# A gated-recurrence block with an MLP on one core: f of the second pair issued from ScalarE's hardware queue, and a new order of the whole program

## The chip, the cores and the metric

The kernel runs on one core of one Trainium2 chip. The metric is the device time of one execution in microseconds; the median of three runs of the kernel before is 179.96 us (179.03 to 180.66).

## What is computed

Two parts follow one another. The first is a recurrence with a gate, for 4 sequences of 768 tokens and 8 heads of width 48; the second is an MLP on the 3072 rows of the result.

```python
f = 1.0 / (1.0 + np.exp(-f_logit))
for t in range(S):
    state = f[:, :, t, :, None] * state + np.einsum('bhd,bhe->bhde', k[:, :, t], v[:, :, t])
    y[:, :, t] = np.einsum('bhd,bhde->bhe', q[:, :, t], state)
...
h = x @ w_in                                  # 3072 x 384 by 384 x 2048
out = (h * (1.0 / (1.0 + np.exp(-h)))) @ w_out  # by 2048 x 384
```

All inputs and the output are float32 in HBM. The kernel computes in bf16 with float32 accumulation.

## The kernel before

The recurrence is done in chunks of 128 tokens. Inside a chunk it becomes masked products of q and k, scaled by running products of f, and between chunks a state of 48 x 48 per head is handed on. There are 24 chunks; the kernel takes them two at a time, as 12 **pairs** (0 to 11). Pairs 0 to 3 hold the first two chunks of one sequence ("T", tokens interleaved, two halves of 64), pairs 4 to 11 one chunk each of two sequences ("N").

Each pair goes through the same steps, and each step is one word in a long string, `PLAN`. A word such as `qg.1.0:G:3` is the step `qg` of pair 1, part 0, on engine G, into buffer 3 of its class. The order of the words is the order of the program: each engine executes its own words in that order, and semaphores do the rest. The letters are P for TensorE (PE), A for ScalarE (ACT), V for VectorE (DVE), G for GpSimd (POOL), and S for SyncE (SP), which only issues DMAs. The steps are:

- `f`, `k`, `q`, `v`: loads of one input for one pair, 384 KB each, line 236; all are issued by SP. f of pair 0 comes in two halves.
- `E`, `L` (ACT): exp and log of f (lines 242, 246, 249). `cs` (PE): running sums (lines 310 to 320). `ia`, `a`, `al` (ACT): exp of them (lines 322, 264, 324).
- `ki`, `qg` (DVE or POOL): k and q times those factors (line 327).
- `tq` (PE) and `qkc` (ACT or DVE): transpose through PE and copy out of PSUM (lines 334, 184/186), or in their place `qkD`: a DMA transpose on SP's queue (line 346).
- `sc` (PE): scores (355, 359). `at` (DVE): mask (363). `vb`: v to bf16 (184/186). `y`, `yi` (PE): the chunk's output (271, 376, 380). `d` (PE), `sd`, `su`: the state handed on (283, 397; 401 or a copy; 407 on POOL).
- `yc`: copy of y out of PSUM. Then `yT` (PE, 388) and `xc` (a copy) transpose it for the MLP, or in their place `yD`, a DMA transpose on SP's queue (392).
- `mi` (PE, 257): x times w_in, eight words for each pair, of six matmuls each; for pairs 0 and 1 each word is two half tiles `mi.P.j.0` and `mi.P.j.1` of 128 columns. `si` (ACT, 262): silu. `mo` (PE, 292): times w_out, four steps for each chunk, step n of which reads part n of w_out. `oc`: copy out. `so`: store, by SP or POOL (302, 304).
- `wi.n`, `wo.n` (214, 217): a quarter of w_in or w_out, issued by POOL with a conversion to bf16. `mi.P.j` reads quarter j/2 of w_in.
- `idle.512.9::7` (448): nine matmuls of 512 columns on zeros into PSUM bank 7, fillers on PE that compute nothing.

Eight PSUM banks and a few buffers of each class are all there is, so a word also waits for the last reader of the buffer that it names. The first four loads of the plan are issued ahead of the masks and constants. ACT has two table sets (exp/log and silu); where consecutive words of ACT need different sets, a table load of 1.28 us stands between (line 497).

The orders of the start that matter here, of the kernel before:

```
SP   f.0.1 f.0.0 f.1.0 k.0.0 q.0.0 q.1.0 k.1.0 v.0.0 f.2.0 v.1.0 k.2.0 q.2.0 v.2.0 f.3.0 f.4.0 k.3.0
POOL qg.1.0 wi.2 ki.1.0 wi.0 vb.0.0 su.0.0 wi.3 su.1.0 wi.1 wo.0 ki.2.0 su.1.1 wo.1 su.0.1 qg.2.1 qg.2.0 ki.2.1 wo.2 wo.3
ACT  E.0.1 L.0.1 E.0.0 L.0.0 E.1.0 ia.0.1 L.1.0 ia.0.0 a.0.1 al.0 a.0.0 ia.1.0 a.1.1 al.1 a.1.0 qkc.0.1 ia.1.1 vb.0.1 ...
PE   idle x10 cs.0 idle x9 cs.1 idle x1 tq.0 idle x4 sc.0 idle x3 tq.1.1 idle x2 tq.1.0 idle x2 d.0 sc.1.0 y.0 sc.1.1 d.1 cs.2 ... mi ...
```

Of the kernel before, what the change touches and what calls it, by code (L numbers as in the profile page):

```python
# [10 lines left out]
F32 = mybir.dt.float32  # L11
# [22 lines left out]

SLOTS = dict(f=4, k=6, q=6, v=6, e=2, lf=3, x=5, qk=5, vb=7, qkT=4, qkTT=2, atm=4, yb=3, xT=4, hT=4, sd=2, al=6, ob=6, pb=8, st0=1, st1=1, st2=1, st3=1)
# [3 lines left out]
f.0.1:S:0 f.0.0:S: f.1.0:S:1 k.0.0:S:0 q.0.0:S:0 E.0.1:A:0 L.0.1:A:0 E.0.0:A: L.0.0:A: q.1.0:S:1 idle.512.10::7 cs.0.1:P:0 cs.0.0:P:1 k.1.0:S:1  # L39
E.1.0:A:1 ia.0.1:A:0 L.1.0:A:1 v.0.0:S:0 ki.0.1:V:0 ia.0.0:A:1 idle.512.9::7 cs.1.0:P:2 a.0.1:A:2 ki.0.0:V:1 f.2.0:S:2 cs.1.1:P:3 al.0:A:0 a.0.0:A:3  # L40
qg.0.1:V: ia.1.0:A:4 qg.0.0:V: a.1.1:A:0 idle.512.1::7 tq.0.1:P:4 v.1.0:S:1 al.1:A:1 a.1.0:A:1 tq.0.0:P:5 qg.1.1:V:2 qkc.0.1:A:0 qg.1.0:G:3 qkc.0.0:V:
k.2.0:S:2 ia.1.1:A:2 wi.2:G: idle.512.4::2 sc.0.0:P:6,7 ki.1.1:V: sc.0.1:P:0,1 q.2.0:S:2 at.0.1.0:V:0 ki.1.0:G: idle.128.3::5 tq.1.1:P:2 vb.0.1:A:0
at.0.0.0:V:1 wi.0:G: at.0.1.1:V: v.2.0:S:2 idle.512.2::5 tq.1.0:P:4 qkc.1.1:V:1 vb.0.0:G:1 qkc.1.0:A: at.0.0.1:V: idle.512.2::6 d.0:P:5,3 E.2.0:A:0
vb.1.1:V:2 sc.1.0:P:0,6 vb.1.0:V:3 y.0:P:1,2 sd.0.0:A:0 at.1.0.0:V:2 L.2.0:A:2 sc.1.1:P:4,7 su.0.0:G:0 at.1.0.1:V: d.1:P:5,0 yc.0.0:A:0 at.1.1.0:V:3
# [4 lines left out]
si.0.5:A: mi.1.7.0:P:7 si.1.0:A:1 mi.0.7.0:P: qg.2.1:G:1 si.1.4:A: mi.0.6.1:P:3 mi.1.6.0:P:6 si.1.5:A: mi.1.6.1:P: si.0.0:A: qg.2.0:G: mi.1.7.1:P:
mi.0.6.0:P: mi.1.2.0:P:0 si.0.6:A: ki.2.1:G: mi.1.3.1:P:2 mi.0.3.1:P:4 si.1.1:A: f.4.0:S:0 mi.0.3.0:P: wo.2:G: mi.0.2.0:P:3 si.0.3:A: tq.2.0:P:5  # L50
si.1.7:A: wo.3:G: mi.1.2.1:P: mi.1.3.0:P: mi.0.2.1:P: tq.2.1:P:4 si.0.2:A: mo.1.1.0:P:7 qkc.2.1:V:0 si.1.6:A: mo.0.0.0:P:3 si.1.3:A: qkc.2.0:V:
si.0.7:A: mo.1.0.0:P:6 k.3.0:S:3 vb.2.0:V:4 si.1.2:A: sc.2.0:P:4,2 sc.2.1:P:5,1 at.2.0.0:V:1 mo.0.1.0:P:0 at.2.1.1:V:0 mo.1.0.1:P: at.2.0.1:V:
# [12 lines left out]
mi.3.4:P:6 qg.6.1:G:3 ia.5.1:A:4 yT.4.0:P:7 al.6.1:A:4 ia.5.0:A:2 d.4.1:P:1 mi.3.2:P:5 xc.4.0:V: E.7.0:A:1 sd.4.1:V:0 v.8.0:S:1 mi.4.0:P:3 ki.5.0:V:0
a.5.0:A:0 ki.6.1:V: mi.4.5:P:7 a.5.1:A:2 qg.5.0:G: ki.6.0:V: al.5.0:A:2 mi.3.0:P:1 mi.3.5:P:4 ki.5.1:G:2 si.3.0:A:3 mi.4.1:P:0 si.3.2:A: su.4.1:G:0
mi.4.6:P:1 si.3.5:A: mi.3.6:P:5 oc.2.0:V:5 qg.5.1:V: tq.5.0:P:4 si.3.6:A: mi.4.3:P:2 qkc.5.0:V:2 si.4.5:A:1 qkD.6.0:S:3 mi.3.1:P:5 si.4.0:A:
vb.6.0:V:2 vb.6.1:V:4 si.3.4:A: mi.4.4:P:7 vb.8.1:V:5 qkD.5.1:S:0 si.4.6:A: mi.4.2:P:4 si.4.1:A: mi.3.7:P:3 si.4.3:A: qkD.6.1:S:1 si.3.1:A: mi.3.3:P:6
# [40 lines left out]
def kernel(  # L109
# [420 lines left out]
```

## Time and profile before

| | |
|---|---|
| median of 3 runs | 179.96 us (179.03 to 180.66) |
| profiled execution, its own time | 180.68 us |
| profiled execution, span from first to last instruction | 178.9 us |
| busy: PE, ACT, DVE, POOL | 171.2, 121.5, 79.4, 63.4 us |
| HBM read, written | 25.17 MB, 4.72 MB |
| line 292 (`mo`) and line 257 (`mi`), all forms | 71.7 and 67.7 us of PE |

The span is what the trace shows from the first to the last instruction; the execution's own time also holds the 1.8 us around it. Of the kernel's chain that ended last, 73% is PE and 10% DMA. In the views below a group's row gives its start, its time, engine, line and tile names; what stands in brackets is how long the engine had been idle and what ended that. "DMA to landing" is the time from the issue of a DMA to the last of its data.

### The profile page before, as it was taken

What the parts mean: (1) busy time and instruction counts of PE and PEld (TensorE: products, weight loads), DVE (VectorE), ACT (ScalarE), POOL (GpSimd) and SP (SyncE); (2) the same over time, 40 slices, a digit from 0 to 9 for tenths busy, and PEclk for the clock granted to TensorE, in tenths of its full rate; (3) what the DMA queues carried; (4) which work ended last, traced back from release to release, by engine and by line L of the source; (5) the groups of instructions that cost most, each with busy time, mean ns of one, the idle gap of its engine ahead of it and who ended that gap; (6) DMA issues with size and microseconds to landing.
All of it is one profiled execution on the core that took longest, in us unless ns stands there. A gap on an engine that the chain in (4) does not pass through costs nothing.

```text
span 178.9 us, 4981 instructions
## 1 busy us (share of the span) xinstructions
PE 171.2 (96%) x2053; PEld 130.3 (73%) x2053; DVE 79.4 (44%) x166; ACT 121.5 (68%) x238; POOL 63.4 (35%) x111
## 2 busy tenths in 40 slices
PE   6997699999999999999999999999999999999993
PEld 2455499966787679976768866768866697888862
DVE  7187910083755958449363078150048654000011
ACT  5677388793599979899979977289840156363620
POOL 6046629702070388300963008621420740000070
PEclk9999789999999999999999999999999999999999
DMA  5999999999999989999879899779994672400053
GB/s 139 286 279 214 252 239 199 238 240 214 202 229 216 189 155 234 150 206 212 175 171 218 165 191 191 171 176 192 223 229 89 126 217 57 122 1 0 4 194 114
DMA packets 108838, 31.84 MB, mean 178 GB/s; under 512 B 102928, under 2 KB 108352, under 8 KB 108816
## 3 DMA queue, kind: packets, MB, share of 16 engines
q1 hardware_dynamic: 104192, 26.12, 70.7%
q0 software_dynamic: 4624, 5.41, 15.2%
q8 instruction: 16, 0.26, 0.6%
q14 instruction: 6, 0.05, 0.1%
HBM read 25.17 MB, written 4.72 MB: 167 GB/s over the span
## 4 chain that ended last, share of the span: by engine, by line
PE 73%; DMA 10%; ACT 6%; SPq 6%; issue 1%; DVE 1%; POOL 0%; ACTq 0%; DVEq 0%
PE pb L257 32%; PE pb L292 29%; DMA v<-in_v_dram 7%; SPq L236 5%; DMA xT<-yb 4%; ACT hT L262 2%; PE pb L359 2%; PE pb L376 2%; ACT x L322 2%; PE pb L380 1%; PE pb L334 1%; PE pb L310 1%; PE pb L388 1%; PE pb L317 1%; PE pb L271 1%
## 5 line engine op out<-in xcount | busy, mean ns | idle before, releaser
L292 PE MATMUL pb<-w_out_sb,hT 128*128 128x384 bf16 (+1 forms) x416 | 71.7, 314 | 0.0
L257 PE MATMUL pb<-xT,w_in_sb 128*128 128x256 bf16 (+1 forms) x672 | 67.7, 258 | 0.3 <-DMA xT<-yb 0.3
L262 ACT ACTIVATE hT<-pb 128x512 bf16<-128x512 f32 x96 | 51.1, 615 | 19.2 <-PE pb L257 18.8
L257 PEld LDWEIGHTS <-w_in_sb 128*128 128x128 bf16 x672 | 57.1, 98 | 7.0 <-issue 0.7
L292 PEld LDWEIGHTS <-hT 128*128 128x128 bf16 x416 | 37.4, 97 | 17.9
L407 POOL TENSOR_TENSOR st<-sd,al 48x192 bf16<-48x192 f32 x40 | 20.5, 513 | 40.5 <-DVE atm L363 12.1
L363 DVE TENSOR_TENSOR atm<-pb,triu 128x512 bf16<-128x512 f32 x32 | 20.1, 684 | 19.2 <-PE pb L359 12.2
L322 ACT ACTIVATE x<-pb 128x384 f32<-128x384 f32 x48 | 22.0, 506 | 9.1 <-PE pb L314 2.8
L327 POOL TENSOR_TENSOR qk<-q,x 128x384 bf16<-128x384 f32 x12 | 12.1, 1015 | 15.6 <-ACT x L322 8.1
L186 DVE COPY ob<-pb 128x384 f32<-128x384 f32 (+1 forms) x12 | 6.4, 537 | 25.1 <-PE pb L292 25.1
L304 POOL DMA_DIRECT2D out_dram<-ob x9 | 5.0, 559 | 28.8 <-ACT ob L184 28.8
L184 ACT COPY ob<-pb 128x384 f32<-128x384 f32 (+1 forms) x14 | 6.2, 449 | 13.2 <-PE pb L292 13.2
L327 POOL TENSOR_TENSOR qk<-k,x 128x384 bf16<-128x384 f32 x9 | 9.6, 1079 | 12.7 <-ACT x L322 7.0
L401 DVE TENSOR_TENSOR sd<-pb,st 128x384 f32<-128x384 f32 x16 | 8.9, 555 | 10.0 <-PE pb L397 4.5
L242 ACT ACTIVATE e<-f 128x768 f32<-128x768 f32 (+1 forms) x13 | 10.3, 792 | 2.7 <-DMA f<-in_f_logit_dram 2.7
L327 DVE TENSOR_TENSOR qk<-k,x 128x384 bf16<-128x384 f32 x15 | 9.8, 668 | 4.8 <-ACT x L322 4.8
L497 ACT ACT_TABLE_LOAD x9 | 11.5, 1283 | 0.2
L448 PE MATMUL pb<-zero,triu 128*128 128x512 bf16 (+1 forms) x31 | 9.5, 445 | 1.4 <-POOL triu masks.py:66 1.4
L363 DVE TENSOR_TENSOR atm<-pb,mask 128x512 bf16<-128x512 f32 x16 | 10.2, 682 | 1.0 <-PE pb L355 0.7
L184 ACT CAST yb<-pb 128x384 bf16<-128x384 f32 x14 | 6.7, 481 | 4.4 <-PE pb L380 2.0
L186 DVE CAST yb<-pb 128x384 bf16<-128x384 f32 x10 | 5.6, 556 | 8.6 <-PE pb L376 2.1
L327 DVE TENSOR_TENSOR qk<-q,x 128x384 bf16<-128x384 f32 x12 | 7.0, 603 | 5.2 <-ACT x L322 3.1
(73 smaller groups left out, 153.1 us busy)
## 6 DMA issues: line engine op xcount, KB each, us to landing
k<-in_k_dram SPq DMA_DIRECT2D x12, 384.0 KB, 5.8
q<-in_q_dram SPq DMA_DIRECT2D x12, 384.0 KB, 6.2
v<-in_v_dram SPq DMA_DIRECT2D x12, 384.0 KB, 5.3
f<-in_f_logit_dram SPq DMA_DIRECT2D x11, 384.0 KB, 5.9
w_in_sb<-in_moe_w_in_dram POOLq DMA_DIRECT2D x4, 384.0 KB, 7.8
w_out_sb<-in_moe_w_out_dram POOLq DMA_DIRECT2D x4, 384.0 KB, 8.7
out_dram<-ob SPq DMA_DIRECT2D x8, 192.0 KB, 3.4
out_dram<-ob POOLq DMA_DIRECT2D x6, 192.0 KB, 2.8
```

The lines of the kernel that those rows point to most:

```text
L184: nc.scalar.copy(dst, src)
L186: ENG[eng].tensor_copy(dst, src)
L242: return nc.scalar.activation(e, at("f", P)[:, j * w:(j + 1) * w], AF.Exp, scale=-1.0)
L257: nc.tensor.matmul(h[:, i, cols], w_in_sb[:, kk, n * 128:(n + 1) * 128], at("xT", P)[:, kk, cols], start=(kk == 0), stop=(kk == KT - 1))
L262: return nc.scalar.activation(at("hT", P)[:, 2 * j:2 * j + 2, :], at("h", P, j).rearrange("p (n c) -> p n c", n=2), AF.Silu)
L292: nc.tensor.matmul(at("o", P, i)[:, cols], at("hT", P)[:, n, i * C:(i + 1) * C], w_out_sb[:, n, cols], start=(n == 0), stop=(n == NT - 1))
L322: nc.scalar.activation(at(kind, P, i).rearrange("p h d -> p (h d)"), at("cs", P, i)[:, 0:HD], AF.Exp, scale=1.0 if kind == "ia" else -1.0)
L327: ENG[eng].tensor_mul(at("qk", P, i)[:, j, :, 0:D], heads("qk"[j], P, i), at("ia" if j else "a", P, i))
L363: ENG[eng].tensor_mul(at("atm", P, i)[:, r], at(f"s{r}", P, i).rearrange("p (n c) -> p n c", c=C), mask[:, None, :].to_broadcast([C, NP, C]))
L407: nc.gpsimd.tensor_mul(at("st", P, i)[lo:lo + D, :, r * D:(r + 1) * D], at("sd", P, i)[lo:lo + D, :, r * D:(r + 1) * D], al_of(P, i)[lo:lo ...
L448: nc.tensor.matmul(buf["pb", int(got)][:, 0:rest[0]], triu, zero[:, 0:rest[0]], start=True, stop=True, skip_group_check=True)
L497: nc.scalar.preload_act_table_set(turns[n])
```

## The change

The loads get an engine of their own choice (`ENG[eng]` in place of `nc.sync`), and the plan is another one. f of pair 1, k of pair 0 and v of pair 0 now carry the letter A: ACT issues them on its own hardware queue. The order of nearly all other words is new, some copies move between ACT and DVE, `yT` and `xc` take the place of `yD` in pairs 5 and 6, and `tq.6.1` with `qkc` takes the place of `qkD`, which in its turn does `2.1`. Fillers: 39 of 512 columns against 28 of 512 and three of 128; seven of them stand ahead of the first `mo`. The orders of the start now:

```
SP   f.0.0 f.0.1 q.0.0 k.1.0 q.1.0 v.1.0 q.2.0 f.2.0 k.2.0 qkD.2.1 v.2.0 f.3.0 f.4.0 f.6.0 k.3.0 q.3.0
POOL qg.1.1 qg.1.0 wi.3 wi.0 su.0.0 wi.1 wi.2 su.1.0 wo.1 su.0.1 wo.0 qg.2.0 wo.2 ki.2.0 vb.2.1 wo.3 vb.2.0
ACT  f.1.0 E.0.1 E.0.0 k.0.0 L.0.0 L.0.1 v.0.0 a.0.0 E.1.0 al.0 a.0.1 L.1.0 ia.0.0 ia.0.1 ia.1.1 ia.1.0 a.1.1 al.1 qkc.0.0 a.1.0
     vb.0.1 vb.0.0 vb.1.1 vb.1.0 sd.0.0 qkc.1.1 E.2.0 yc.0.0 L.2.0 yc.0.1 xc.0.0 ia.2.1 a.2.1 xc.0.1 yc.1.0 yc.1.1 ...
DVE  qg.0.0 qg.0.1 ki.0.0 ki.0.1 ki.1.1 ki.1.0 qkc.0.1 at.0 x4 qkc.1.0 sd.1.0 at.1 x4 qg.2.1 ki.2.1 sd.1.1 xc.1.0 ...
PE   idle x16 cs.0 idle x9 cs.1 tq.0 idle x4 sc.0.1 tq.1.1 sc.0.0 d.0 d.1 tq.1.0 idle x2 y.0 sc.1.0 yi.0.1 sc.1.1 yT.0.0 cs.2 yT.0.1
     idle x1 y.1 mi.0.6.0 mi.0.7.1 yi.1.1 yT.1.0 mi.0.7.0 mi.0.6.1 yT.1.1 mi.1.7.0 ... (27 half tiles, tq.2.0) idle x7 mo.1.0.0 mo.1.1.0
     mo.0.0.0 mi.0.4.0 mo.1.1.1 sc.2 mo.1.1.2 ...
```

The code around the plan, cut:

```diff
+GROUPS = [(0,), (1,), (2,), (3,), (4,), (5,), (6,), (7,), (8,), (9,), (10,), (11,)]
+JOINT = ()
+WI_CUT = [0, 2, 4, 6, 8]
 PLAN = """
-f.0.1:S:0 f.0.0:S: f.1.0:S:1 k.0.0:S:0 q.0.0:S:0 E.0.1:A:0 L.0.1:A:0 E.0.0:A: L.0.0:A: q.1.0:S:1 idle.512.10::7 cs.0.1:P:0 cs.0.0:P:1 k.1.0:S:1
+f.0.0:S:0 f.0.1:S: q.0.0:S:0 f.1.0:A:1 k.1.0:S:0 q.1.0:S:1 E.0.1:A:0 E.0.0:A: k.0.0:A:1 v.1.0:S:0 L.0.0:A:0 L.0.1:A: v.0.0:A:1 idle.512.16::7
...
-                w = d_ff // parts
-                nc.gpsimd.dma_start(out=w_in_sb[:, :, n * w:(n + 1) * w], in_=w_in_src[:, :, n * w:(n + 1) * w])
+                cols = slice(256 * WI_CUT[n], 256 * WI_CUT[n + 1])
+                nc.gpsimd.dma_start(out=w_in_sb[:, :, cols], in_=w_in_src[:, :, cols])
...
-            return nc.sync.dma_start(out=dst, in_=src)
+            return ENG[eng].dma_start(out=dst, in_=src)
```

With these values of `GROUPS`, `JOINT` and `WI_CUT` the tiles, the slices of the weights and the matmuls of `mi`, `si` and `mo` are the same as before; the new words `ac` and `am` do not occur in the plan.

More of the change, by code (lines that the diff above doesn't have):

```diff
@@ L41 @@
[L41 to L44, printed above, removed]
@@ L49 @@
[L49 to L52, printed above, removed]
@@ L65 @@
[L65 to L68, printed above, removed]
@@ new lines @@
+cs.0.0:P:0 cs.0.1:P:1 a.0.0:A:0 q.2.0:S:2 E.1.0:A:1 qg.0.0:V:0 al.0:A:0 a.0.1:A:1 L.1.0:A:1 qg.0.1:V:1 ia.0.0:A:2 idle.512.9::7 cs.1.1:P:2 f.2.0:S:2
+ia.0.1:A:3 ki.0.0:V: cs.1.0:P:3 ki.0.1:V: ia.1.1:A:4 tq.0.0:P:4 ia.1.0:A:0 ki.1.1:V:2 tq.0.1:P:5 a.1.1:A:1 ki.1.0:V:3 al.1:A:1 k.2.0:S:2 qkc.0.0:A:0
+qkc.0.1:V: qg.1.1:G: a.1.0:A:2 idle.512.4::1 sc.0.1:P:6,7 vb.0.1:A:0 qg.1.0:G: tq.1.1:P:0 vb.0.0:A:1 at.0.1.1:V:0 vb.1.1:A:2 sc.0.0:P:1,2 vb.1.0:A:3
+wi.3:G: d.0:P:5,4 at.0.0.1:V:1 sd.0.0:A:0 d.1:P:3,7 at.0.0.0:V: wi.0:G: qkc.1.1:A:1 tq.1.0:P:2 at.0.1.0:V: su.0.0:G:0 E.2.0:A:0 qkc.1.0:V:
@@ new lines @@
+idle.512.2::5 y.0:P:5,1 sd.1.0:V:1 wi.1:G: sc.1.0:P:0,6 yc.0.0:A:0 yi.0.1:P: L.2.0:A:2 at.1.0.1:V:2 wi.2:G: sc.1.1:P:2,3 yT.0.0:P:5 at.1.0.0:V:
+yc.0.1:A:1 su.1.0:G:0 cs.2.0:P:6 xc.0.0:A:0 at.1.1.0:V:3 cs.2.1:P:1 at.1.1.1:V: wo.1:G: yT.0.1:P:0 ia.2.1:A:3 a.2.1:A:4 idle.512.1::5 y.1:P:5,2
+xc.0.1:A: qg.2.1:V:4 mi.0.6.0:P:3 yc.1.0:A:2 ki.2.1:V: mi.0.7.1:P:0 yi.1.1:P: sd.1.1:V:0 yT.1.0:P:5 qkD.2.1:S:0 mi.0.7.0:P: yc.1.1:A:0 xc.1.0:V:1
+mi.0.6.1:P: al.2:A:2 sd.0.1:V:1 yT.1.1:P:7 mi.1.7.0:P:2 su.0.1:G:0 v.2.0:S:2 xc.1.1:A: mi.1.0.0:P:5 ia.2.0:A:0 mi.0.0.1:P:1 f.3.0:S:3 a.2.0:A:1
@@ new lines @@
+mi.1.1.0:P:4 wo.0:G: mi.1.0.1:P: mi.1.7.1:P: qg.2.0:G:0 mi.0.0.0:P: mi.1.6.0:P:7 si.0.0:A:0 mi.1.1.1:P: wo.2:G: mi.0.3.0:P:6 si.1.1:A:1 mi.1.6.1:P:
+mi.1.2.1:P:1 si.1.0:A: ki.2.0:G: mi.0.3.1:P: si.0.7:A: mi.1.2.0:P: mi.0.1.0:P:4 si.1.2:A: mi.1.3.1:P:5 mi.0.1.1:P: f.4.0:S:0 mi.0.5.0:P:0 si.0.1:A:
+mi.1.3.0:P: mi.0.5.1:P: si.0.3:A: mi.1.4.0:P:1 si.0.6:A: tq.2.0:P:4 si.1.3:A: mi.0.4.1:P:6 mi.1.5.0:P:3 qkc.2.0:A: mi.0.2.0:P:5 mi.1.5.1:P:
+mi.1.4.1:P: si.1.5:A: mi.0.2.1:P: si.0.2:A: si.0.5:A: si.1.6:A: si.1.7:A: idle.512.7::4 mo.1.0.0:P:4 si.1.4:A: mo.1.1.0:P:3 mo.0.0.0:P:5 f.6.0:S:1
@@ L129 @@
     NT = d_ff // 128
+    W = 2 * C * max(len(g) for g in GROUPS)
+    first_of = {P: g[0] for g in GROUPS for P in g}
+    col_of = {P: 2 * C * k for g in GROUPS for k, P in enumerate(g)}
     sb = ctx.enter_context(tc.tile_pool(name="sb", bufs=1))
@@ L251, in emit @@
             j = rest[1]
+            x = at("xT", first_of[P])
+            if P in JOINT:
+                for kk in range(KT):
+                    nc.tensor.matmul(at("h", P, j), w_in_sb[:, kk, j * 128:(j + 1) * 128], x[:, kk], start=(kk == 0), stop=(kk == KT - 1))
+                return
             h = at("h", P, j).rearrange("p (n c) -> p n c", n=2)
@@ L256, in emit @@
                 for kk in range(KT):
-                    nc.tensor.matmul(h[:, i, cols], w_in_sb[:, kk, n * 128:(n + 1) * 128], at("xT", P)[:, kk, cols],
+                    nc.tensor.matmul(h[:, i, cols], w_in_sb[:, kk, n * 128:(n + 1) * 128], x[:, kk, col_of[P] + cols.start:col_of[P] + cols.stop],
                                      start=(kk == 0), stop=(kk == KT - 1))
@@ L261, in emit @@
             j = rest[1]
-            return nc.scalar.activation(at("hT", P)[:, 2 * j:2 * j + 2, :], at("h", P, j).rearrange("p (n c) -> p n c", n=2), AF.Silu)
+            hT = at("hT", first_of[P])
+            if P in JOINT:
+                return nc.scalar.activation(hT[:, j], at("h", P, j), AF.Silu)
+            return nc.scalar.activation(hT[:, 2 * j:2 * j + 2, col_of[P]:col_of[P] + 2 * C], at("h", P, j).rearrange("p (n c) -> p n c", n=2), AF.Silu)
         if kind == "al" and T:
@@ L291, in emit @@
             for n in range(4 * rest[2], 4 * rest[2] + 4):
-                nc.tensor.matmul(at("o", P, i)[:, cols], at("hT", P)[:, n, i * C:(i + 1) * C], w_out_sb[:, n, cols], start=(n == 0), stop=(n == NT - 1))
+                nc.tensor.matmul(at("o", P, i)[:, cols], at("hT", first_of[P])[:, n, col_of[P] + i * C:col_of[P] + (i + 1) * C], w_out_sb[:, n, cols], start=(n == 0), stop=(n == NT - 1))
         elif kind == "oc":
@@ L363, in emit @@
             ENG[eng].tensor_mul(at("atm", P, i)[:, r], at(f"s{r}", P, i).rearrange("p (n c) -> p n c", c=C), mask[:, None, :].to_broadcast([C, NP, C]))
+        elif kind == "ac":
+            nc.scalar.copy(at("atm", P, i)[:, rest[2]], at(f"s{rest[2]}", P, i).rearrange("p (n c) -> p n c", c=C))
+        elif kind == "am":
+            m = at("atm", P, i)[:, rest[2]]
+            if T:
+                for g in range(2):
+                    mm = m[g * HC:(g + 1) * HC].rearrange("p n (s c) -> p n s c", s=2)
+                    nc.gpsimd.affine_select(out=mm, in_=mm, compare_op=mybir.AluOpType.is_ge, fill=0.0, base=-i, pattern=[[0, NP], [i, 2], [1, HC]], channel_multiplier=-1)
+            else:
+                nc.gpsimd.affine_select(out=m, in_=m, compare_op=mybir.AluOpType.is_ge, fill=0.0, base=0, pattern=[[0, NP], [1, C]], channel_multiplier=-1)
         elif kind in ("y", "yi"):
@@ L412, in takes @@
     def takes(kind, rest):
-        if kind in ("wi", "wo", "so", "yi", "idle"):
+        if kind in ("wi", "wo", "so", "yi", "am", "idle"):
             return []
```

117 lines of the change are left out of this document (59 added, 58 removed).

## The prediction

> **What bounds the kernel now.** I read the page, then busy time by stretches of the first 36 us, then the timeline of that start, then single DMAs.
>
> ```profile
> span 178.9 us, 4981 instructions
> PE 171.2 (96%) x2053; PEld 130.3 (73%) x2053; DVE 79.4 (44%) x166; ACT 121.5 (68%) x238; POOL 63.4 (35%) x111
> ```
>
> ```profile
> 17.60:18.90 1.30, 0.03 (x4) 0.00 (x0) 0.67 (x3) 0.69 (x2) 1.23 (x3) 1.00 1.14 297
> 18.90:20.00 1.10, 0.70 (x16) 0.44 (x16) 1.10 (x3) 0.00 (x0) 0.21 (x1) 0.94 1.21 232
> 20.00:23.00 3.00, 2.90 (x52) 2.20 (x51) 2.44 (x6) 1.45 (x3) 2.35 (x4) 0.50 1.19 248
> 26.00:35.40 9.40, 9.40 (x172) 9.40 (x170) 0.36 (x1) 7.51 (x14) 8.09 (x11) 1.00 1.25 215
> ...
> 60.00:80.00 20.00, 20.00 (x271) 16.45 (x270) 12.12 (x24) 18.36 (x39) 9.47 (x14) 1.00 1.07 188
> ```
>
> The columns are length; busy time of PE, PEld, DVE, ACT, POOL; granted clock; DMA share; GB/s. PE has no hole from 26 us on, so in the middle only added PE work or a new wait can move the end. The recoverable time is ahead of 23 us: PE does nothing from 17.6 to 18.9, little until 20, and then runs 20 to 23 at a clock of 0.50 (1.5 us lost in these 3 us). The cause of the hole:
>
> ```profile
> 3.37 0.52 ACT L242 ACTIVATE e<-f 128x384 f32<-128x384 f32 x1 [1.35 <-DMA f<-in_f_logit_dram]
> 4.36 0.51 ACT L242 ACTIVATE e<-f 128x384 f32<-128x384 f32 x1
> 6.77 2.11 PE L448 MATMUL pb<-zero,triu 128*128 128x512 bf16 x9
> 6.77 0.84 ACT L242 ACTIVATE e<-f 128x768 f32<-128x768 f32 x1 [1.35 <-DMA f<-in_f_logit_dram]
> 7.52 0.47 ACT L322 ACTIVATE x<-pb 128x384 f32<-128x384 f32 x1
> 8.06 0.56 DVE L327 TENSOR_TENSOR qk<-k,x 128x384 bf16<-128x384 f32 x1 [3.85 <-ACT x L322]
> 8.62 0.86 ACT L322 ACTIVATE x<-pb 128x384 f32<-128x384 f32 x2
> 10.96 1.09 ACT L184 COPY qkTT<-pb 128x1024 bf16<-128x1024 bf16 x1
> 11.22 1.00 POOL L327 TENSOR_TENSOR qk<-q,x 128x384 bf16<-128x384 f32 x1 [7.31 <-ACT x L322]
> 11.35 0.69 DVE L186 COPY qkTT<-pb 128x1024 bf16<-128x1024 bf16 x1
> 12.14 0.64 PE L355 MATMUL pb<-qkTT 48*64 48x128 bf16 x32
> 12.17 0.95 POOL L214 DMA_DIRECT2D w_in_sb<-in_moe_w_in_dram  x1
> 13.42 0.51 ACT L184 CAST vb<-v 128x384 bf16<-128x384 f32 x1 [0.97 <-DMA v<-in_v_dram]
> 16.65 0.64 PE L271 MATMUL pb<-vb,atm 64*128 64x48 bf16 x32
> 18.23 0.63 DVE L186 CAST vb<-v 128x384 bf16<-128x384 f32 x2 [1.55 <-DMA v<-in_v_dram]
> 18.77 2.48 DVE L363 TENSOR_TENSOR atm<-pb,mask 128x512 bf16<-128x512 f32 x4
> 22.38 0.77 POOL L217 DMA_DIRECT2D w_out_sb<-in_moe_w_out_dram  x1
> 23.19 0.48 ACT L184 CAST yb<-pb 128x384 bf16<-128x384 f32 x1 [0.26 <-PE pb L271]
> 28.36 0.79 POOL L217 DMA_DIRECT2D w_out_sb<-in_moe_w_out_dram  x1
> 35.46 2.11 PE L292 MATMUL pb<-w_out_sb,hT 128*128 128x384 bf16 x12
> ```
>
> v of pair 1 stands tenth on SP's queue, behind f of pair 2, and lands at 18.2; pair 1's `vb`, `at` and `d` all wait for it. Then the output products (`mo`) begin with a margin, as the weights are in time:
>
> ```profile
> 25.85 0.17 PE pb L388 x3
> 26.02 7.71 PE pb L257 x138
> 33.73 0.45 PE pb L334 x8
> ...
> 175.83 0.32 ACT ob L184
> ```
>
> ```profile
> DMA to landing us min/median/max: 6.7/6.7/6.7
> DMA to landing us min/median/max: 10.6/10.6/10.6
> DMA to landing us min/median/max: 7.6/7.6/7.6
> ```
>
> These are single weight DMAs: the first (issued 12.17, landed 18.9), the fifth (22.38, landed 33.0) and the sixth (28.36, landed 36.0). `mo` needs the fifth (`wo.0`) at 35.5.
>
> **The change, by parts.** The whole order is new, so I put both orders on one scale: T, the start of the first `mo`, and the PE work still to do at T.
>
> *PE work.* Four more blocks go through PE (`yT`) in place of a DMA transpose (`yD`): 4 x 0.17 = 0.68 us, all on the path, since PE has no hole there. At the first `mo` the new order still owes one half tile of `mi` (six 128-column products, 7.71 x 6/138 = 0.34) and one transposed block (0.45) that before had done. So a T of 35.5 - 0.34 - 0.45 - 0.68 = **34.0** would give the old time; every us later costs one.
>
> *The start.* f.1.0 leaves SP's queue, as do k.0.0 and v.0.0; v.1.0 becomes the sixth issue on SP. Both v are among the first eight loads; before, the eighth load was v.0.0, landed at 13.4. So pair 1's v is there near 14, not 18.2. An early f.1.0 buys nothing itself: its E now stands behind a.0.0 on ACT. What it costs is issue time on ACT, which no row shows. The SP row of three f issues gives 0.5 us each if ACT stands still, 0 if the issue runs beside an activation:
>
> ```profile
> 0.74 1.56 SPq L236 DMA_DIRECT2D f<-in_f_logit_dram  x3
> ```
>
> Bounds are 0 and 1.5 us, 0.5 taken: four half E and L from 4.36 end at 6.5 plus 0.5 = 7.0. The 16 fillers say the same: ten took 4.45 us from 1.37, the nine later ones 2.11:
>
> ```profile
> 1.37 4.45 PE L448 MATMUL pb<-zero,triu 128*128 128x512 bf16 x10 [1.37 <-POOL triu masks.py:66]
> ```
>
> so they end near 7.1 to 7.4 and `cs.0.0` by 7.5. ACT then runs a, E, al, a, L, four ia, a, al, qkc, a: seven x of 0.43 (the row of two), E and L 0.75 each (6.77 to 7.52), qkc 1.0, al 0.1 twice, together 5.7, to 13.2, or 13.65 with a.1.0 itself. On DVE, ki.0.1, ki.1.1 and ki.1.0 (0.56 each) follow ia.0.1 at 10.8, then qkc (0.69) to 13.4 with a short wait for ACT; `sc` takes 0.3, so the first `at` starts at 13.75, four at 0.62 end at 16.25, and y.0 runs at 16.8 against 16.65 before. No wait for v follows: qkc, sd and four more `at` end at 20.2. ACT, from its sd.0.0 at 15.4, has qkc, E, then from 17.6 yc, L, yc, xc, two x, xc and two yc (0.43 to 0.75 each) until 21.9, and the last yT follows. So `mi` runs without holes from about 22.5 with four half tiles done. Then 27 half tiles (9.1) and one transposed block (0.45) end at 32.0, and seven new fillers (7 x 0.23 = 1.6, hidden by nothing unless PE waits anyway) bring T to **33.6** if no weight is late. That alone would be 0.4 us faster.
>
> *The weights.* POOL's first weight now stands behind qg.1.1 and qg.1.0 (1.0 each). The second follows a.1.0: 13.65 + 1.0, so the first weight is issued at 14.7 instead of 12.17. wo.1 now stands ahead of wo.0, so the first `mo` needs the sixth weight, not the fifth. How fast do they come?
>
> ```profile
> q0 software_dynamic: 2120, 1.83, 70.2%
> q1 hardware_dynamic: 5737, 1.78, 51.7%
> ```
>
> This is the DMA view of 20 to 36 us: 1.83 MB are 4.65 weights of 393 KB, one per 3.44 us beside the loads; they held the engines 70.2% of 16 us, so 2.41 us each when alone. Late bound: 14.7 + 6.7 + 5 x 3.44 = 38.6. Early bound: two us less for the first (the row's 6.7 had loads queued ahead) and 2.41 for each: 14.7 + 4.7 + 12.05 = 31.5. What lies between: SP's queue now stops at the transpose qkD.2.1 until ki.2.1 is done near 22, and its eleven loads are down by about 18, so two weights can come alone, 19.4 and 21.8, and four beside loads, 13.8 more: 35.6. I take **T = 35.5**, nearer to the late bound's rate because the loads behind qkD.2.1 are then all queued. The other weights are used earlier by PE than before, too, but a wait there is spent before the same T. The PE clock in that wait is costed at nothing.
>
> *The rest.* ACT gets five xc, three vb, a yc and a qkc more, five oc and an sd less: about 2.6 us. In 60 to 80 us ACT is busy 18.36 of 20 us, so 1.6 us are free there; costed at nothing, up to 1 us if it bunches. Other copies trade DVE and ACT. Four yD fewer ease SP. Offsets of the weight slices are the same numbers.
>
> **The sum.** 35.5 - 34.0 = 1.5 us later: the span goes from 178.9 to 180.4. The profiled execution took 180.68 with its ends, 0.7 over the median of 179.96; carried to the median, **181.5 us**.
>
> **Rivals.** *The weights are in time*: the silence of SP's queue gives them the engines, T = 33.6, 0.4 us faster, 179.6. For it: 2.41 us each by the engine time; against: later issue, one more ahead.
>
> *Clearly faster*: weights near the early bound, and the fillers mark waits that shrink further, as the eight loads land before they are asked for. My walk holds 2.7 us in which PE waits (1.5 ahead of y.0, 1.2 from there to 22.5); with 1.6 of them gone, T = 32.0: 2.0 us faster, 178.0. Against it is the DVE chain to y.0, no faster than before.
>
> *Slower by the clock*: the wait at the first `mo` comes on top of seven fillers. Before, two holes of 1.3 and 0.4 us were followed by 3 us at 0.50. If a wait of 2 us does the same here, another 1.5 to 1.7 us go: 1.5 + 1.7 = 3.2, so 183.2. It decides once the wait passes about 1.5 us. The Trainium skill ("TensorE: Matmul & The Clock Gate", "What's actually happening") wants about 3.4 us of idle for that; here less was enough, so the measurement speaks for the rival.
>
> *The second queue delays the first load*: if f.1.0 takes turns with f.0's halves, f.0 is complete up to one load later, and a load takes (13.4 - 6.77)/5 = 1.3 us. The first chain, the weights' issue and T all move by 1.3: 1.5 + 1.3 = 2.8, so 182.8. Against: f.1.0 may be issued only behind the table load,
>
> ```profile
> 0.74 1.28 ACT L466 ACT_TABLE_LOAD   x1 [0.74 <-PEq L514]
> ```
>
> at 2.0, when f.0 is half down. The Trainium skill ("DMA: Bandwidth & Descriptors", "Queues, rings and completion order") says that the engines take turns between queues packet by packet; by that rule a second queue brings no bandwidth and can only delay f.0, which no run here shows yet.
>
> **How the numbers follow.** Forecast 0.32 (its own range 180.3 to 182.6, T from 34.3 to 36.6); weights in time 0.23; clearly faster 0.17; clock 0.16; f.0 delayed 0.12. A measurement of this kernel tells about 1% (1.8 us) from no change. Slower by over 1% is above 181.76: both slow rivals (0.28) and 0.13 of the forecast, 0.41. Faster is below 178.16: 0.16 of the fast rival. The rest, 0.43, is the same. The range of 178.0 to 183.6 leaves out half of the fast rival and the late bound (38.6, 184.6).
>
> **What would show it.** PE's hole at 17.6 to 19.5 and the half clock at 20 to 23 are gone, and vb.1.1 no longer waits for a DMA. The first weight is issued at 14.7. PE idles behind the seven fillers, released by the DMA of w_out_sb, and the first `mo` starts at 35.5. From there to the last matmul lie 140.3 + 1.5 us (before: 35.5 to 175.8). I am wrong if `mo` starts before 33.6 or after 37, or if PE shows holes of over 1 us behind it.

## The result, and the profile after

| | before | after |
|---|---|---|
| median of 20 runs each, taken together | 179.93 us (177.66 to 181.00) | 180.92 us (180.58 to 184.84) |
| profiled execution, its own time | 180.68 us | 180.86 us |
| profiled execution, span | 178.9 us | 179.1 us |

The ratio of after to before is 1.0113, 95% interval 1.0088 to 1.0137. The ratios here and below compare undisturbed runs alone, so they can differ from the quotient of the medians.

So the kernel became slower by 1.0 us in the medians. The two profiled executions differ by 0.2 us only: the one of before is among its longer runs, 0.75 us over its median, the one of after lies on its median. From the page of the kernel after, span and busy time of each engine:

```profile
span 179.1 us, 5004 instructions
PE 173.5 (97%) x2074; PEld 130.8 (73%) x2077; DVE 79.1 (44%) x167; ACT 123.5 (69%) x242; POOL 62.7 (35%) x111
```

Busy time by stretches, of the kernel after (length; busy time of PE, PEld, DVE, ACT, POOL; granted clock; DMA share; GB/s):

```profile
16.00:17.60 1.60, 1.45 (x53) 1.11 (x57) 1.60 (x4) 1.55 (x3) 1.50 (x4) 1.00 0.54 66
17.60:18.90 1.30, 1.26 (x40) 0.88 (x32) 1.24 (x3) 1.30 (x3) 1.30 (x3) 1.00 1.25 195
...
20.00:23.00 3.00, 2.88 (x72) 2.64 (x72) 2.62 (x6) 2.08 (x7) 1.02 (x2) 1.00 1.11 160
```

The hole of PE at 17.6 and the half clock at 20 to 23 us are gone. What is new is in the first row: the DMA engines are half idle, at 66 GB/s, while SP's queue stands at the transpose of pair 2. The timeline of the start, of the kernel after (ACTq and SPq are the sequencers that issue DMAs):

```profile
0.77 0.48 ACTq L246 DMA_DIRECT2D f<-in_f_logit_dram  x1
1.38 6.25 PE L477 MATMUL pb<-zero,triu 128*128 128x512 bf16 x16 [1.38 <-POOL triu masks.py:66]
3.12 2.38 SPq L246 DMA_DIRECT2D q<-in_q_dram  x1
5.52 0.52 ACT L252 ACTIVATE e<-f 128x384 f32<-128x384 f32 x1 [3.50 <-DMA f<-in_f_logit_dram]
5.53 0.46 ACTq L246 DMA_DIRECT2D k<-in_k_dram  x1
...
6.49 0.38 ACTq L246 DMA_DIRECT2D v<-in_v_dram  x1
13.61 1.79 ACT L194 CAST vb<-v 128x384 bf16<-128x384 f32 x4
14.80 1.72 POOL L224 DMA_DIRECT2D w_in_sb<-in_moe_w_in_dram  x2
16.88 0.57 PE L289 MATMUL pb<-vb,atm 64*128 64x48 bf16 x32
21.92 2.29 SPq L364 DMA_TRANSPOSE qkTT<-qk  x1
24.21 0.79 POOL L227 DMA_DIRECT2D w_out_sb<-in_moe_w_out_dram  x1
```

All four casts of v run in one piece without a wait. The chain that ended last, of the kernel after (start, length, what), goes through the sixth weight to the first `mo`:

```profile
14.80 6.04 DMA w_in_sb<-in_moe_w_in_dram
...
24.21 9.83 DMA w_out_sb<-in_moe_w_out_dram
34.08 2.11 PE pb L310 x12
...
176.22 0.32 ACT ob L194
```

And the DMA view of the kernel after for 18 to 34 us, and then for 26 to 34 us alone (queue: packets, MB, share of the engines' time; q0 carries POOL's weights, q1 SP's loads):

```profile
q0 software_dynamic: 2703, 2.35, 101.5%
q1 hardware_dynamic: 1270, 0.34, 20.5%
```

```profile
q0 software_dynamic: 1330, 1.00, 89.1%
q1 hardware_dynamic: 1270, 0.34, 41.0%
```

2.35 MB are six weights of 0.393 MB in 16 us, one per 2.7 us. The second view shows that these 16 us have two parts. All 1270 packets of SP's queue fall behind 26 us: until then the weights had the engines to themselves and moved 1.35 MB in 8 us, one per 2.3 us. From 26 us on the two queues moved nearly the same number of packets, 1330 and 1270, and the weights slowed to 1.00 MB in 8 us, one per 3.1 us.

### The profile page after: what moved, and what is told of

It reads as the page before. It is cut to its first block, busy times and chain, and to the rows that moved or that the text cites. A ratio compares the mean times of both kernels' runs of the same rounds, so it can differ in the third digit from the quotient of the medians.

```text
span 179.1 us, 5004 instructions
## 1 busy us (share of the span) xinstructions
PE 173.5 (97%) x2074; PEld 130.8 (73%) x2077; DVE 79.1 (44%) x167; ACT 123.5 (69%) x242; POOL 62.7 (35%) x111
## 4 chain that ended last, share of the span: by engine, by line
PE 82%; DMA 9%; ACT 4%; issue 1%; DVE 1%; POOL 1%; DVEq 0%; POOLq 0%; ACTq 0%
PE pb L310 35%; PE pb L272 30%; DMA w_out_sb<-in_moe_w_out_dram 5%; PE pb L477 3%; DMA w_in_sb<-in_moe_w_in_dram 3%; PE pb L377 2%; ACT x L340 2%; PE pb L409 2%; PE pb L405 2%; PE pb L352 2%; PE pb L335 1%; PE pb L417 1%; PE pb L426 1%; DVE qk L345 1%; PE pb L373 1%
## 5 line engine op out<-in xcount | busy, mean ns | idle before, releaser
L272 PE MATMUL pb<-xT,w_in_sb 128*128 128x256 bf16 (+1 forms) x672 | 69.0, 257 | 0.4 <-ACT al L342 0.3
L196 DVE COPY ob<-pb 128x384 f32<-128x384 f32 (+1 forms) x17 | 9.0, 538 | 28.2 <-PE pb L310 20.5
L381 DVE TENSOR_TENSOR atm<-pb,mask 128x512 bf16<-128x512 f32 x16 | 10.2, 684 | 16.3 <-PE pb L373 16.2
L322 POOL DMA_DIRECT2D out_dram<-ob x8 | 4.4, 559 | 28.4 <-DVE ob L196 24.9
L477 PE MATMUL pb<-zero,triu 128*128 128x512 bf16 x36 | 11.7, 467 | 1.5 <-POOL triu masks.py:66 1.4
L345 POOL TENSOR_TENSOR qk<-k,x 128x384 bf16<-128x384 f32 x8 | 8.0, 1005 | 11.8 <-ACT x L340 6.0
L196 POOL CAST vb<-v 128x384 bf16<-128x384 f32 x7 | 3.8, 550 | 21.9 <-DMA v<-in_v_dram 21.8
L194 ACT COPY ob<-pb 128x384 f32<-128x384 f32 (+1 forms) x9 | 3.9, 432 | 8.9 <-issue 4.9
L345 DVE TENSOR_TENSOR qk<-k,x 128x384 bf16<-128x384 f32 x16 | 9.1, 594 | 1.1 <-ACT x L340 1.1
L194 ACT CAST yb<-pb 128x384 bf16<-128x384 f32 x15 | 7.2, 481 | 3.3 <-PE pb L409 1.4
```

The source lines that it names most:

```text
L194: nc.scalar.copy(dst, src)
L196: ENG[eng].tensor_copy(dst, src)
L272: nc.tensor.matmul(h[:, i, cols], w_in_sb[:, kk, n * 128:(n + 1) * 128], x[:, kk, col_of[P] + cols.start:col_of[P] + cols.stop], start=(kk ...
L345: ENG[eng].tensor_mul(at("qk", P, i)[:, j, :, 0:D], heads("qk"[j], P, i), at("ia" if j else "a", P, i))
L381: ENG[eng].tensor_mul(at("atm", P, i)[:, r], at(f"s{r}", P, i).rearrange("p (n c) -> p n c", c=C), mask[:, None, :].to_broadcast([C, NP, C]))
L477: nc.tensor.matmul(buf["pb", int(got)][:, 0:rest[0]], triu, zero[:, 0:rest[0]], start=True, stop=True, skip_group_check=True)
```

## The experiments

Each was run together with the kernel before. "After" and "before" in the headings name the kernel that was edited. Beside the first four, the next four, the next three and the last, the kernel before had medians of 180.47, 180.16, 179.05 and 179.32 us; ratios are to it. So times of different groups are compared by their ratios, not by their medians.

**1. Before, profiled again, nothing changed.**

> The kernel before once more, for a second profile. Theory A (the start of before differs from run to run: v of pair 1 and the half clock that follows its hole): time near the median of 179.9, and where it is below 180.7 the first mo lies as much ahead of 35.46 us; the work from the first mo to the last matmul stays at 140.4 us. Theory B (the two kernels differ in the middle): first mo at 35.4 to 35.5 again, and the difference lies behind it.

Measured: 181.11 us, ratio 1.0009 (0.9968 to 1.0051); profiled execution 181.03 us. The chain of that second profile:

```profile
34.58 1.95 PE pb L292 x12
...
176.18 0.32 ACT ob L184
```

By stretches, of the same execution:

```profile
17.60:18.90 1.30, 0.55 (x11) 0.43 (x13) 1.30 (x3) 0.00 (x0) 0.83 (x2) 0.81 1.15 240
```

The hole was there again, PE busy for 0.55 of 1.30 us. `mo` began 0.88 us earlier than in the first profile and the end was 0.35 us later: T alone doesn't fix the end; the middle of this kernel varies by about a microsecond between executions. The same kernel had medians of 181.11 and 180.47 us side by side, so a difference of 0.6 us between two medians says nothing by itself. Both profiles of before are of executions above the 179.93 us of the first table, so what its shorter runs do differently stays open.

**2. Before, v of pair 1 issued ahead of f of pair 2.**

```diff
-... v.0.0:S:0 ... f.2.0:S:0 ... v.1.0:S:1
+... v.0.0:S:0 ... v.1.0:S:1 f.2.0:S:0 ...
```

> Before, with v of pair 1 issued ahead of f of pair 2 and nothing else. Theory A (the late v costs before its hole and the half clock): v lands near 14.6, PE has no hole at 17.6 and no half clock at 20 to 23, the first mo moves from 35.46 to between 32.3 and 33.0 (wo.0 landed at 33.0), so 2 us off the time: 177.5 to 178.3. Theory B (the weights or ACT take it back): first mo not before 34.5, 179.3 or more.

Measured: 180.76 us, ratio 1.0003 (0.9967 to 1.0039). The chain of this kernel:

```profile
10.62 8.27 DMA f<-in_f_logit_dram
...
23.10 8.96 DMA w_in_sb<-in_moe_w_in_dram
...
35.85 1.95 PE pb L292 x12
```

No gain. The wait for v is gone and the wait for f of pair 2, now one place later, stands where it was: PE idles 1.83 us until 20.17. The granted clock stayed at 1.00 all the same, and T is no earlier without the half clock, because the chain to it goes through a quarter of w_in that lands at 32.06. So the late v, which the prediction made the cause of the hole, was only the load that happened to stand there. That the loads as a whole come too slowly is the reading that fits, and experiment 6 bears it out.

**3. After, without the seven fillers ahead of the first `mo`.**

```diff
-idle.512.7::4
```

> After, without the seven fillers ahead of the first mo. Theory A (the first mo waits for wo.0, landed at 34.04): the wait takes their place, first mo at 34.0, 180.6 to 181.1. Theory B (the fillers are on the path): first mo at 32.3, 1.5 us less, 179.3.

Measured: 181.02 us, ratio 1.0085 (1.0035 to 1.0134), profiled execution 180.80 us. The timeline of this kernel:

```profile
33.86 2.12 PE L310 MATMUL pb<-w_out_sb,hT 128*128 128x384 bf16 x12 [1.28 <-DMA w_out_sb<-in_moe_w_out_dram]
```

The wait for the weight takes the fillers' place. They cost nothing that these runs show.

**4. After, without these fillers, and wo.0 ahead of wo.1.**

```diff
-wo.1:G: ... wo.0:G:
+wo.0:G: ... wo.1:G:
-idle.512.7::4
```

> After, without the seven fillers and with wo.0 issued ahead of wo.1. Theory A (weights bound the start of mo one after the other): wo.0 lands near 31.4, first mo at 32.2, but the first product with wo.2 (landed at 37.0, wanted 1.8 us earlier) then waits 1.2: in all 0.7 us less, 180.2. Theory B (only wo.0 counts): 1.9 us less, 179.0.

Measured: 181.82 us, ratio 1.0055 (1.0017 to 1.0092); the profiled execution, 182.87 us, is the longest of its runs, so its timeline is read for the places of the waits only:

```profile
32.81 2.11 PE L310 MATMUL pb<-w_out_sb,hT 128*128 128x384 bf16 x12
36.75 0.81 PE L310 MATMUL pb<-w_out_sb,hT 128*128 128x384 bf16 x4 [1.49 <-DMA w_out_sb<-in_moe_w_out_dram]
39.67 1.62 PE L310 MATMUL pb<-w_out_sb,hT 128*128 128x384 bf16 x9 [1.54 <-DMA w_out_sb<-in_moe_w_out_dram]
```

The first `mo` starts 1.3 us earlier, and PE then waits for the next two weights instead.

**5. After, with f of pair 1 issued by SP again.**

```diff
-f.1.0:A:1
+f.1.0:S:1
```

> After, with f of pair 1 back on SP's queue (its fourth issue) and nothing else: the change's title undone in the new order. Theory A (the second queue only delays f of pair 0, landed at 5.5 instead of 4.25, and sixteen fillers on PE hide that): E of pair 0 starts near 4.4 instead of 5.5, the first sums still wait for the fillers until 7.5, the first mo at 34 again, 180.6 to 181.2. Theory B (the ACT queue brings the loads in sooner): pair 1's inputs come a load later and the time rises by 1 us, to 182.

Measured: 182.51 us (180.05 to 183.33), ratio 1.0084 (1.0044 to 1.0123). The chain of its profiled execution, 0.8 us over its median:

```profile
24.44 12.09 DMA w_out_sb<-in_moe_w_out_dram
...
36.56 2.11 PE pb L310 x12
```

The sixth weight is issued 0.2 us later than in the kernel after and lands 2.5 us later. But the twelve runs fall in two groups, 180.05 to 181.19 and 182.42 to 183.33 us, and the profile is of the longer group. The ratio of 1.0084 is a little under the 1.0113 of the kernel after, and the two intervals overlap, so a worth of this one letter in the new order isn't shown. Nor does the edit take the second queue away: ACT still issues k and v of pair 0, and the rate of 6 to 15 us stays at 320 GB/s, against 325 in the kernel after. The new order without any load on ACT's queue was not run.

**6. Before, with only f of pair 1 issued by ACT.** The title of the change, in the old order; the code around the plan is that of the kernel after, which with these values makes the same tiles and matmuls.

```diff
-f.1.0:S:1
+f.1.0:A:1
```

> Before's order, with f of pair 1 issued by ACT and nothing else. Theory A: the second half of f of pair 0 lands near 5.5, the first sums run 0.5 to 1 us later, E of pair 1 no longer waits until 6.77; in all within 0.5 us of before. Theory B (the queue speeds the start): 1 us less than before.

Measured: **178.11 us** (177.67 to 179.99), ratio 0.9921 (0.9884 to 0.9958): faster than before by 2.0 us in the medians and by 1.4 us in the ratio. Against the kernel after, with its 1.0113, that is 1.9%. By stretches, of this kernel:

```profile
6.00:15.00 9.00, 7.77 (x103) 4.93 (x104) 5.50 (x9) 6.92 (x16) 3.42 (x4) 1.00 1.17 325
17.60:18.90 1.30, 1.11 (x35) 0.75 (x34) 1.30 (x3) 1.21 (x3) 1.22 (x3) 1.00 1.16 284
20.00:23.00 3.00, 3.00 (x82) 2.94 (x80) 1.51 (x4) 2.58 (x8) 2.00 (x3) 1.00 1.20 251
2.00:42.00 40.00, 37.18 (x620) 27.80 (x621) 19.98 (x51) 29.29 (x56) 19.41 (x33) 1.00 1.20 255
```

The same of before, and the last stretch of after:

```profile
6.00:15.00 9.00, 8.32 (x108) 5.11 (x107) 5.83 (x10) 6.18 (x14) 3.75 (x4) 1.00 1.07 279
2.00:42.00 40.00, 37.24 (x597) 27.22 (x596) 19.57 (x50) 28.81 (x55) 18.44 (x31) 0.96 1.16 243
```

```profile
2.00:42.00 40.00, 38.97 (x600) 27.36 (x602) 17.32 (x44) 30.56 (x60) 16.33 (x29) 1.00 1.14 226
```

With one load on a second queue the rate of 6 to 15 us rises from 279 to 325 GB/s (283 in the second profile of before, 326 in experiment 9), the hole and the half clock go, and the chain says what that is worth:

```profile
33.05 1.95 PE pb L309 x12
...
173.31 0.32 ACT ob L193
```

T is 2.41 us earlier than in the first profile of before and the end 2.52; against the second profile it is 1.53 and 2.87. The new order, in its turn, moves less in its first 42 us than before did: (243 - 226) x 40 us = 0.68 MB, nearly two loads.

**7. After, with f of pair 1 on SP, eleven first fillers instead of 16, and none ahead of `mo`.**

```diff
-f.1.0:A:1 ... idle.512.16::7 ... idle.512.7::4
+f.1.0:S:1 ... idle.512.11::7
```

> After, with f of pair 1 on SP's queue, eleven first fillers instead of sixteen and without the seven ahead of mo. Theory A (the whole start, the issue of the weights in it, hangs on f of pair 0 and the fillers): first sums at 6.1 instead of 7.5, first weight issued at 13.5, the first mo and the end 1.2 us earlier, 179.5. Theory B (the DMA engines bound the weights, whenever they are issued): first mo at 34 again, 180.8.

Measured: 182.81 us (180.50 to 185.75), ratio 1.0124 (1.0066 to 1.0182). From the timeline of this kernel:

```profile
14.38 1.72 POOL L224 DMA_DIRECT2D w_in_sb<-in_moe_w_in_dram  x2
33.73 2.12 PE L310 MATMUL pb<-w_out_sb,hT 128*128 128x384 bf16 x12 [1.76 <-DMA w_out_sb<-in_moe_w_out_dram]
```

The earlier f of pair 0 does not bring the weights forward by its 1.2 us: the first is issued 0.4 us earlier, as the other loads come later. This profile is of the shortest of six runs, and its T is 0.35 us ahead of that of the kernel after. The 16 fillers of the changed kernel are not what holds it.

**8. After, with the first weight issued between the two `qg`, without the seven fillers.**

```diff
-qg.1.1:G:... qg.1.0:G:... wi.3:G:
+qg.1.1:G:... wi.3:G: qg.1.0:G:...
-idle.512.7::4
```

> After, without the seven fillers and with the first weight issued between POOL's two qg of pair 1, so at 13.6 instead of 14.8. Theory A (the weights set the start of mo, and the DMA engines stand half idle at 16 to 17.6 us): each weight lands about 1.1 us earlier, first mo at 32.9 and 1.1 us less time, 179.8. Theory B (weights are bound by the rate of the engines from 18 us on, or another wait follows): within 0.4 us of after, 180.5 to 181.2.

Measured: 184.56 us, ratio 1.0198 (1.0135 to 1.0261). The timeline of this kernel:

```profile
36.29 3.49 PE L310 MATMUL pb<-w_out_sb,hT 128*128 128x384 bf16 x12 [3.88 <-DMA w_out_sb<-in_moe_w_out_dram]
```

The first weight is issued earlier, at 13.71, and the sixth lands 2.2 us later. Between 26 and 34 us the weights moved 0.63 MB here, against 1.00 MB in the kernel after. The order of issue doesn't explain it: SP's next two loads were issued ahead of the sixth weight in experiments 5 and 8, with the first `mo` at 36.6 and 36.3, but also in experiment 3, with the first `mo` at 33.86. Why the sixth weight is so late here stays open.

**9. Experiment 6 with wo.1 ahead of wo.0.** The order of the two weights alone, in the best version.

```diff
-wo.0:G: ... wo.1:G:
+wo.1:G: ... wo.0:G:
```

> Before's order with f of pair 1 issued by ACT (which alone took 178.1) and, on top, wo.1 issued ahead of wo.0, as the new order has it. Theory A (what the new order loses is that the first mo needs the sixth weight): wo.0 lands where the sixth did, at 34.7, instead of 32.1; the first mo waits, 33.05 to 34.7, and 1.6 us are added: 179.7. Theory B (PE work and waits in the middle are the loss): no change, 178.1.

Measured: 180.11 us, ratio 1.0081 (1.0046 to 1.0116). The timeline of this kernel:

```profile
35.22 2.12 PE L309 MATMUL pb<-w_out_sb,hT 128*128 128x384 bf16 x12 [2.10 <-DMA w_out_sb<-in_moe_w_out_dram]
```

Making the first `mo` need the sixth weight costs 2.2 us of T and, against experiment 6, 1.6% of the time by the two ratios. (This profile is of a run 0.55 us over its median, so T may be earlier in a typical one.) This one step undoes the whole gain of the queue.

**10. After, with wo.0 and wo.1 both ahead of su.0.1, wo.0 first, no seven fillers, and a later place for one `mo`.**

```diff
-wo.1:G: ... su.0.1:G:0 ... wo.0:G: ... idle.512.7::4 ... mo.1.1.2:P: ... mo.0.0.1:P:
+wo.0:G: wo.1:G: ... su.0.1:G:0 ... mo.0.0.1:P: mo.1.1.2:P:
```

> After, with wo.0 issued ahead of wo.1 and both ahead of POOL's su.0.1, the seven fillers left out, and the first product with wo.2 moved behind mo.0.0.1. Theory A: wo.0 lands near 31.5, first mo at 32.3, wo.1 is issued ahead of SP's next loads and lands by 34.3, in time; 1.7 us less than after, 179.2, and the runs above 181.5 go. Theory B: the weights are bound by the engines' rate and only the next wait shows, 180.5 or more.

Measured: 180.31 us (180.13 to 180.66), ratio 1.0084 (1.0057 to 1.0112). The timeline of this kernel:

```profile
32.16 2.11 PE L310 MATMUL pb<-w_out_sb,hT 128*128 128x384 bf16 x12
37.46 1.46 PE L310 MATMUL pb<-w_out_sb,hT 128*128 128x384 bf16 x8 [0.22 <-DMA w_out_sb<-in_moe_w_out_dram]
39.85 0.52 PE L301 MATMUL pb<-vb,qk 64*128 64x96 bf16 x16 [0.93 <-POOL vb L196]
```

T is 1.9 us earlier and 0.5 us remain of it at the end: PE waits for another weight and then for v of pair 2, which is issued at 23.4 and lands 14.6 us later. The long runs of the kernel after, up to 184.84 us, are absent from these twelve, as theory A said.

**11. After, with `yD` again for pairs 5 and 6.**

```diff
-yT.5.0 yT.5.1 yT.6.0 yT.6.1 (PE) and their xc
+yD.5.1:S:2 yD.5.0:S: yD.6.0:S:0 yD.6.1:S:
```

> After, with the outputs of pairs 5 and 6 transposed by DMA again: four yT and four xc out, four yD on SP's queue in. Theory A (PE has no hole in the middle, each yT is on the path): 0.7 us less, 180.2. Theory B (mi of pairs 5 and 6 then waits for the DMA transposes, or SP's loads of pairs 7 and 8 come late): the same as after or up to 1 us more.

Measured: 184.39 us, ratio 1.0325 (1.0264 to 1.0386); the span is 182.6 us, 3.5 longer than after. The timeline of this kernel:

```profile
93.19 0.83 PE L272 MATMUL pb<-xT,w_in_sb 128*128 128x256 bf16 x6 [1.82 <-DMA xT<-yb]
100.93 1.25 PE L272 MATMUL pb<-xT,w_in_sb 128*128 128x256 bf16 x10 [1.77 <-DMA xT<-yb]
```

With the `yD` at these places of the new order PE waits for two DMA transposes, and the 0.68 us of `yT` buy 3.5 us of span.

**12. Experiment 10 with v of pair 2 issued ahead of the DMA transpose of pair 2.**

```diff
-qkD.2.1:S:0 ... v.2.0:S:2
+v.2.0:S:2 qkD.2.1:S:0
```

> The reordered changed kernel (a_order), with one word moved: SP issues v of pair 2 ahead of its DMA transpose for pair 2, which waits for a product of POOL until 22.2 us. Theory A (what a_order lost to its two waits, 0.38 us at 36.9 and 1.09 us at 38.6, was v of pair 2 standing in the queue behind that transpose): v is issued before 15 us and lands before 22; both waits go, the first mo stays at 32.2 to 32.6, since only one load of 1.2 us comes ahead of the first weights; span 178.5 - 1.5 = 177.0, 178.8 us beside 180.3 for a_order. Theory B (a load gained for v is a load lost for the weights): every weight lands 1.2 us later, the first mo waits to 33 and the fourth output weight is waited for at 37 to 38 as before; 180 us or more, no gain. A is wrong if PE still stands over 0.5 us between 36 and 40; B is wrong if the first mo starts before 32.7 and the time is below 179.5.

Measured: 180.45 us (180.23 to 180.59), ratio 1.0063 (1.0037 to 1.0089); profiled execution 180.35 us, against 180.34 for experiment 10. Timeline of this kernel, PE and then ACT:

```profile
32.10 2.11 PE L310 MATMUL pb<-w_out_sb,hT 128*128 128x384 bf16 x12
37.71 1.46 PE L310 MATMUL pb<-w_out_sb,hT 128*128 128x384 bf16 x8 [0.54 <-DMA w_out_sb<-in_moe_w_out_dram]
42.00 0.48 PE L328 MATMUL pb<-lf,tincl 128*128 128x384 bf16 x2 [0.58 <-ACT lf L256]
40.00 0.84 ACT L252 ACTIVATE e<-f 128x768 f32<-128x768 f32 x1 [3.35 <-DMA f<-in_f_logit_dram]
```

Neither theory held whole: the first `mo` starts in time and v is no longer waited for, as A said, and the time doesn't move, as B said. The weight is 0.3 us later, and the next load of SP's queue, f of pair 3, has taken v's place. Waits of 0.22 + 0.93 us became 0.54 + 0.58 here. What the stop of SP's queue does to the engines can be read from the stretch of 15 to 24 us, in experiment 10 and then in this one:

```profile
15.00:24.00 9.00, 8.57 (x214) 7.05 (x210) 7.58 (x14) 7.76 (x18) 7.33 (x12) 1.00 1.02 159
15.00:24.00 9.00, 8.72 (x212) 7.03 (x207) 7.50 (x14) 7.75 (x17) 7.32 (x12) 1.00 1.15 201
```

One load ahead of the stop fills the gap that the stop had left (237 GB/s at 16 to 17.6 us, against 50), so the gap is the stop's doing; but filling it with one load gained no time. Moving several was not tried.

## Why the prediction was right or wrong

The time was forecast at 181.5 and came out at 180.92, but that it came so near is in part luck, as errors cancel: T was 1.4 too late in the forecast, the stretch from T to the last matmul was 0.3 longer than forecast, and the step from the profile of before to the median took off 0.7 that was not there for the kernel after. The stretch behind the last matmul is 0.2 shorter. 181.5 - 1.4 + 0.3 + 0.7 - 0.2 = 180.9. In the profiles themselves the change cost 0.2 us of span, 178.9 to 179.1, where 1.5 were forecast, and T lies just outside the forecast's own 34.3 to 36.6.

- **The start: right in its times, wrong in its cause.** The first weight issued at 14.80 (14.7 forecast), y.0 at 16.88 (16.8), the end of the first fillers at 7.63 (`cs.0` by 7.5). The hole and the half clock went, as forecast. But the step "an early f.1.0 buys nothing itself" failed: by itself, on ACT's queue, it buys 1.4 to 2.0 us in the old order (6), and the moved v, to which I gave the credit, buys nothing by itself (2). I priced that load by who reads it; its worth was in how fast all the loads behind it arrive. (The count of eight loads was off as well: v of pair 0 is the ninth issue now, with the two halves of f counted as before.)
- **DMA issues on ACT: mis-sized.** 0.5 us was taken, with bounds 0 and 1.5. The timeline of after shows the issue of k at 5.53 beside the E at 5.52, and the one of f inside the table load: no ACT time. The lower bound held.
- **f of pair 0 delayed: the rival was right about the load and wrong about the price.** The first half E starts at 5.52 instead of 3.37, but `cs.0` comes as forecast, since 16 fillers hold PE until 7.6 anyway, and experiment 7 shows no clear gain from undoing it.
- **The weights: the right mechanism, T mis-sized.** `mo` does wait for the sixth weight behind the fillers; at 34.08, not 35.5. The first landed 6.0 us after its issue, within the bounds, and the five others took 34.04 - 20.84 = 13.2 us, 2.64 each. I had the first landing at 19.4, one more at 2.41 and four at 3.44, 16.2 us for the five. Both rates were near: one weight per 2.3 us alone and per 3.1 us beside SP's loads. What I had wrong is how long the weights stay alone: I let SP's loads come back near 22 us. The transpose was issued then, at 21.92, but that alone took 2.29 us, the next load was issued at 24.26, and that queue moved nothing between 18 and 26. The rival "the weights are in time" had that effect right, and T lies between its 33.6 and my 35.5.
- **The break-even of 34.0: useful, with a scatter.** After: T 0.08 over it, end 0.39 later. Between experiment 6 and before T and the end moved alike (2.41 and 2.52), between 9 and 6 by 2.17 and 2.48 (end 175.79). In the second profile of before it failed by 1.2.
- **The clock rival fell.** In experiment 9 PE waited 2.10 us and the twelve products behind took 2.12 us, full pace. In experiment 8 it waited 3.88 us and they took 3.49. The Trainium skill ("TensorE: Matmul & The Clock Gate", "What's actually happening") wants about 3.4 us of idle; these two waits agree with it, and the two short holes of before (1.3 and 0.4 us) don't. In experiment 2 a single hole of 1.83 us left the clock at 1.00. So what the two short holes did in both profiles of before isn't explained, and I had let them speak for the rival. In the kernel after the fillers cover the wait and the clock stays at 1.00.
- **`yT` on the path: incomplete as a trade.** No run isolates its cost of 0.68 us; the `yD` that it replaces, put back, costs 3.5 us in this order (11). The profile lists one wait of PE behind T, of 0.26 us, so the sign "holes of over 1 us" did not come.
- **The base.** I worked the sum against one profiled execution and took off 0.7 to come to the median. The profile of before was of one of the longer runs of a kernel whose runs spread by 3.3 us; that of after sat on its median. About 0.75 of the measured 1.0 us is the distance of that profile from its median, and what before's typical run looks like inside isn't shown.

Put together: the queue gains 1.4 to 2.0 us in the old order, by experiment 6. The new order ends 2.9 us later than that, profile against profile (176.22 against 173.31). Its T is 1.03 later, it owes 0.34 + 0.45 more at T, and `yT` adds 0.68, which is 2.5; 0.4 remains unassigned. That the weight order alone can make such a loss is shown by 9; that putting it right in the new order returns only 0.5 is shown by 10, and in 4, 10 and 12, whichever transfer is moved ahead, the next one is waited for. I read this as transfers that are late as a body between 16 and 40 us. That the stop of SP's queue leaves the engines half idle is shown by 12 (159 against 201 GB/s); that this idle time is what makes the new order slower is argued from the 226 GB/s, not shown.

## What to carry to other kernels

When several loads are late in a row, moving one of them only renames the wait: look at the bytes per second of the whole stretch, and at what keeps a queue from issuing. Try the smallest part of a change alone, in the old order, before a new order is built round it: here the one letter in the plan beat both kernels. Compare against several executions of the kernel before, as one profile can lie 0.75 us from its median.

## What was unexpected of the hardware

- **A second hardware queue raised the rate of the first loads**, from 279 to 325 GB/s in 6 to 15 us, with the same loads in the program. The two queues hardly ran side by side: in experiment 6 ACT's load moved its 0.39 MB ahead of 6 us, and 2.91 MB of the 2.93 MB of 6 to 15 us came through SP's queue alone. Why that queue runs without gaps once a load has left it isn't shown. The Trainium skill ("DMA: Bandwidth & Descriptors", "Issuing engines are not separate DMA queues") says that issuing from several engines saves only the sequencer's time, usually small; by that the letter would be worth little, and here it was worth 1.4 to 2.0 us.
- **POOL's weights and SP's loads shared packets evenly, not bytes**: from 26 to 34 us the weights had 1330 packets and SP's loads 1270, but 1.00 MB against 0.34 MB, as a packet of a weight held about 750 bytes and one of a load about 270. That makes a load beside weights slow: v of pair 2, issued at 24.26, took 13.7 us to land, and 14.57 us in experiment 10.
- **Issuing a DMA from ACT took no time of ACT**, 0.38 to 0.48 us each on its sequencer, beside running activations.
